# FNet mixing beside a ReLU MLP on one Trainium2 core: two neighbouring quarters of the second transform's operands made in one step each, and the order of block 8 to the end written anew

## The chip, the cores and the metric

The kernel runs on one core of a Trainium2 chip. Its five engines each take their instructions in the order in which they were issued, and wait for one another through semaphores: TensorE (PE; its weight loads are shown as PEld), VectorE (DVE), ScalarE (ACT), GpSimd (POOL) and SyncE (SP). In this kernel SP and POOL only issue DMAs, except for some reductions on POOL. The metric is the device time of one execution in microseconds; three runs of the kernel before took 1236.45, 1238.53 and 1238.07 us, with a median of 1238.07 us.

## The reference

The input x has 2048 rows of 576 numbers. It is normalised along its rows (xn), and the output is the sum of x, of the real part of a two-dimensional Fourier transform of xn, and of a two-layer perceptron with 4608 hidden units:

```python
a = einsum("bsd,ed->bse", xn, dft_hid_re)            # hidden transform
b = einsum("bsd,ed->bse", xn, dft_hid_im)
y = einsum("ts,bse->bte", dft_seq_re, a) - einsum("ts,bse->bte", dft_seq_im, b)
h = maximum(einsum("bsd,df->bsf", xn, w1), 0)
out = x + y + einsum("bsf,fd->bsd", h, w2)
```

The transforms are given as dense matrices, and the kernel works them out as matrix products.

## The kernel before

Every matrix product of two float32 operands is made of three float16 passes. An operand v is split into a high part, which ACT makes by a rounding copy, and a low part, which DVE makes as v minus the high part; the passes are high by high, high by low and low by high. Nearly all products also go through a 2 by 2 block scheme with seven products in place of eight (Strassen's, in Winograd's form): besides the four blocks of an operand it needs sums of blocks, which DVE makes, and its results are added up as they leave PSUM.

The work comes in nine blocks of the perceptron (0 to 8), in which the weights, the hidden layer and the second product of one ninth of the hidden units are worked through. In the last of them the operands of the transforms are prepared too. Behind it comes the hidden transform, whose results stay in the chip as sixteen 128-row tiles (they are taken in two turns of eight), and then the sequence transform in sixteen units of seven products each, eight units after either turn.

The order from block 8 to the end isn't left to a scheduler. It stands in two strings of words, `BLOCK8` and `TURN`; each word names a step and its arguments, the program runs through them one after the other, and so the order of the words is the order of the instructions on each engine. The steps of which the texts speak are these; lines are those of the kernel before.

- `p:g:i:n` seven-product matmuls of the first layer (PE, L710); `f` brings a product out of its bank, `h` and `l` make the high (ACT, L719) and low part (DVE, L723) of the hidden layer, `r` applies the ReLU to a sum block (L739), `x` and `y` make sums of blocks (DVE, L743 to L745 and L748), `H` and `L` the high (ACT, L751) and low part (DVE, L757) of these sums.
- `m:g:n` is product n of the second layer for group g: 12 matmuls of 128x288 (PE, L807). `e:g:n` brings it out: `:A` on ACT (L821), `:V` on DVE (L823), others as an addition on DVE (L825). `a` adds the result to the output in memory by a DMA from POOL (L832).
- `F` loads a block of the sequence matrix (SP, L1229) and `S` takes its column sums of magnitudes (ACT, L1236); `dl` loads the hidden transform's matrix for its maxima (SP, L348), which `dx` takes (DVE, L392). `dh` and `dw` make high (ACT, L1200) and low parts (DVE, L1206) of the hidden transform's operands.
- `q:t:z:n` is product n of the hidden transform for tile t (7 matmuls of 128x288; PE, L1389), and `c:t:z:n` collects it into a buffer of float32 blocks `tb` (DVE, L1402; ACT, L1404).
- A tile in `tb` has four 288-wide blocks b11, b12, b21, b22. `sh:t:s` and `sl:t:s` write the high part (ACT, L1358) and low part (DVE, L1362) of them as operands `R` of the sequence transform: s is 11, 21 or 22 for one block of 288, and 0 for the four sums together (1152). `rs:t` makes these four sums in place (DVE, L1368 to L1371), in which the blocks are overwritten; so `sh` and `sl` of 11, 21 and 22 come before it, those of 0 after it.
- `cl:n:q` loads a block of the sequence matrix for unit n, `os` makes sums of these blocks (DVE, L1444), `oh:m` and `ol:m` make the high (ACT, L1013) and low part (DVE, L1017) of left operand number m. `u:n:i:h` is half h of product i of unit n: 12 matmuls of 128x288 (PE, L1475), over four tiles; half 0 takes the tiles 0, 2, 1, 3 and half 1 the tiles 4, 6, 5, 7. Unit 0's product i uses operand number i. `ue` brings a product out (L1487 to L1491), `ua` writes it out by a DMA.

For each tile half of a product the three matmuls are, in this order, high by high, high (left) by low (R), and low (left) by high (R):

```python
for k in range(HK)[ks]:
    r = right_of(kh * HK + RANK[k])
    for j, (a, c) in enumerate(((0, 0), (0, 1), (1, 0))):
        nc.tensor.matmul(ps, w[:, a, RANK[k]], r[:, c, RIGHT[rq]], ...)
```

Of the kernel before, what the change touches and what calls it, by code (L numbers as in the profile page):

```python
# [9 lines left out]
F16 = mybir.dt.float16  # L10
# [4 lines left out]
ALU = mybir.AluOpType  # L15
# [3 lines left out]
P = 128  # L19
S = 2048  # L20
# [21 lines left out]
SB = 2 * EH  # L42
# [98 lines left out]
p:31:1:4 l:31:1:11 h:31:1:22 a:30:1 dl:0 e:30:3:V F:32:0 p:32:0:1 f:31:1:3 h:31:1:12 l:31:1:12  # L141
r:31:1 m:30:4 f:32:0:1:V f:32:0:2 L:31:0 p:32:0:6 e:30:4 p:32:0:5 f:32:0:6:A l:31:1:22 a:30:4
m:30:5 x:31:1 y:31:1 f:32:0:5:A m:30:6 H:31:1 e:30:5 a:30:5 L:31:1 p:32:0:3 h:32:0:11 dl:1
p:32:1:1 l:32:0:11 dx:0:0 p:32:1:2 e:30:6:V S:32:0 m:31:0 dx:0:1 a:30:6 F:32:1 f:32:0:3 p:32:0:7
f:32:1:1:V r:32:0 f:32:1:2 p:32:1:6 h:32:1:11 f:32:0:7 l:32:1:11 h:32:0:22 p:32:1:5 x:32:0
f:32:1:6:A p:32:1:7 l:32:0:22 e:31:0:A m:31:1 f:32:1:5:V f:32:1:7 h:32:1:22 l:32:1:22 p:32:1:4
e:31:1 p:32:1:3 h:32:1:12 a:31:1 dl:2 l:32:1:12 m:31:3 f:32:1:3 dx:1:1 r:32:1 x:32:1 p:32:0:4
dx:1:0 p:33:0:5 h:32:0:12 m:31:2 l:32:0:12 f:33:0:5:A y:32:0 y:32:1 H:32:0 p:33:0:1 e:31:2:V
S:32:1 p:33:1:1 f:33:0:1:V L:32:0 e:31:3:A m:31:4 F:33:0 H:32:1 f:33:1:1:V m:31:5 e:31:4 L:32:1
a:31:4 dl:3 m:31:6 e:31:5 dx:2:1 a:31:5 m:32:0 e:31:6:V S:33:0 dx:2:0 a:31:6 p:33:1:6 F:33:1  # L150
m:32:1 f:33:1:6:V p:33:0:3 p:33:0:2 p:33:0:6 f:33:0:2 e:32:0:A p:33:1:2 f:33:0:6:V dL:0:0
h:33:0:11 f:33:0:3 m:32:2 f:33:1:2 r:33:0 e:32:1 h:33:1:11 l:33:1:11 a:32:1 p:33:0:7 l:33:0:11
dx:3:1 p:33:1:7 f:33:0:7 m:32:3 x:33:0 h:33:0:22 e:32:2:A l:33:0:22 dx:3:0 p:33:0:4 p:33:1:5
y:33:0 h:33:0:12 dR:0 l:33:0:12 H:33:0 m:32:4 f:33:1:5:V dp:0 S:33:1 f:33:1:7 L:33:0 p:34:0:1
e:32:3:A dL:0:1 p:33:1:4 f:34:0:1:A e:32:4 dh:0:0:1 p:33:1:3 h:33:1:12 dw:0:0:1 a:32:4 h:33:1:22
m:32:5 l:33:1:12 dh:0:0:0 f:33:1:3 F:34:0 r:33:1 dw:0:0:0 p:34:0:5 e:32:5 m:32:6 l:33:1:22
a:32:5 ds:0:0 dh:0:1:1 m:33:0 dh:0:1:0 dw:0:1:1 dh:0:0:2 x:33:1 p:34:0:6 e:32:6:A p:34:0:2
dh:0:0:3 f:34:0:5:V a:32:6 dw:0:0:2 m:33:1 dw:0:0:3 S:34:0 f:34:0:2 dL:0:2 p:34:0:3 f:34:0:6:V
# [118 lines left out]
def kernel(  # L277
# [44 lines left out]
    NS = 7  # L322
# [1279 lines left out]
```

## Time and profile before

| | |
|---|---|
| runs | 1236.45, 1238.53, 1238.07 us (median 1238.07) |
| profiled execution | 1237.58 us, of which the span from the first to the last instruction is 1235.8 us |
| mean granted clock of TensorE | 0.999 |
| busy | PE 1211.6 us (98%), DVE 1061.7 us (86%), ACT 722.7 us (58%), POOL 213.6 us (17%) |

The profile comes from one execution of its own. A busy time is the sum over an engine's instructions, as the profiler recorded them; weight loads of PE overlap its matmuls. In a timeline a row gives the start, the duration, the engine, the line, the operation with the tiles that it writes and reads, the shapes, the number of like instructions that the row stands for, and in brackets the time for which the engine stood idle ahead of it with what ended that. Numbers at the end of buffer names are left out there. Times count from the first instruction.

### The profile page before, as it was taken

The numbers are of one execution on the slowest core, as the hardware profiler recorded it, in microseconds if no ns is written. First come the engines' busy times: TensorE is split into PE (matmuls) and PEld (weight loads), VectorE is DVE, ScalarE is ACT, GpSimd is POOL, SyncE is SP. The second block draws the span as 40 slices with busy tenths as digits, with TensorE's granted clock in tenths as the row PEclk, the third lists the DMA queues.
The fourth block names the chain that finished last, engine by engine and source line by source line (L and its number), as shares of the span: only waits on it lengthen the run. The fifth ranks groups of instructions, "written<-read, shape, count | busy, mean of one in ns | idle before, by whom it ended". The sixth has DMA issues, their size and how long they took to land.

```text
span 1235.8 us, 26013 instructions
## 1 busy us (share of the span) xinstructions
PE 1211.6 (98%) x10394; PEld 993.7 (80%) x10394; DVE 1061.7 (86%) x2046; ACT 722.7 (58%) x1256; POOL 213.6 (17%) x279
## 2 busy tenths in 40 slices
PE   6999999999999999999999999999999999999998
PEld 6856878888888888888888888877777777777777
DVE  7967999988898888988988889999977769987885
ACT  6665776765766666667667546666444445534342
POOL 2641112122213122222121111100111110000000
PEclk9999999999999999999999999999999999999999
DMA  7997468778777778676667577630755532255441
GB/s 227 206 183 171 152 136 169 166 138 164 151 164 142 173 140 181 134 145 139 141 129 156 129 182 165 122 96 26 210 121 142 122 91 49 78 168 173 147 131 35
DMA packets 127050, 175.96 MB, mean 142 GB/s; under 512 B 48336, under 2 KB 88784, under 8 KB 126928
## 3 DMA queue, kind: packets, MB, share of 16 engines
q1 hardware_dynamic: 97696, 121.99, 33.5%
q0 software_dynamic: 28672, 51.92, 28.4%
q8 instruction: 81, 1.33, 0.4%
q10 hardware_dynamic: 560, 0.39, 0.1%
q14 instruction: 41, 0.34, 0.1%
HBM read 112.53 MB, written 56.62 MB: 137 GB/s over the span
## 4 chain that ended last, share of the span: by engine, by line
PE 87%; DVE 6%; DMA 2%; issue 2%; ACT 1%; POOL 1%; SPq 1%; POOLq 0%; DVEq 0%; ACTq 0%
PE bank L710 26%; PE p L807 26%; PE p L1475 26%; PE pd L1389 7%; PE p L847 1%; PE p L586 1%; DMA raw_w<-in_w_dram 1%; DVE R L1362 1%; DMA accs<-in_x_dram 1%; DMA x<-in_x_dram 0%; DMA xT<-wbuf 0%; DVE st L471 0%; DVE wbuf L923 0%; ACT dbuf L511 0%; DVE cs L1017 0%
## 5 line engine op out<-in xcount | busy, mean ns | idle before, releaser
L807 PE MATMUL p<-w2s,h 128*128 128x288 f16 x2688 | 357.1, 286 | 0.6 <-ACT dbuf L821 0.6
L1475 PE MATMUL p<-R,cs 128*128 128x288 f16 x2688 | 331.0, 286 | 2.5 <-DVE cs L1017 2.5
L1475 PEld LDWEIGHTS <-cs 128*128 128x128 f16 x2688 | 262.8, 98 | 69.6 <-DVE cs L1017 3.4
L807 PEld LDWEIGHTS <-h 128*128 128x128 f16 x2688 | 263.0, 98 | 62.8 <-issue 0.8
L710 PEld LDWEIGHTS <-dbuf 128*128 128x128 f16 x1568 | 153.2, 98 | 24.8 <-issue 4.7
L710 PEld LDWEIGHTS <-wbuf 128*128 128x128 f16 x1568 | 153.4, 98 | 20.3
L1013 ACT ACTIVATE cs<-tb,sc_c 128x1024 f16<-128x1024 f32 x56 | 64.3, 1148 | 82.4 <-PE p L1475 58.0
L710 PE MATMUL bank<-xT,dbuf 128*128 128x256 f16 x896 | 109.9, 273 | 1.2 <-ACT accs L700 1.0
L710 PE MATMUL bank<-xT,wbuf 128*128 128x256 f16 x896 | 110.3, 273 | 0.0
L1017 DVE SCALAR_TENSOR_TENSOR cs<-tb,sc_c,cs 128x1024 f16<-128x1024 f32 x56 | 71.7, 1283 | 22.2 <-ACT cs L1013 21.4
L832 POOL DMA_DIRECT2D spill<-dbuf x70 | 61.1, 913 | 166.9 <-DVE dbuf L825 124.0
L710 PE MATMUL bank<-accs,dbuf 128*128 128x256 f16 x672 | 85.9, 273 | 2.4 <-DVE accs L734 1.7
L710 PE MATMUL bank<-accs,wbuf 128*128 128x256 f16 x672 | 85.9, 273 | 0.0
L1013 ACT ACTIVATE cs<-accs,sc_c 128x1024 f16<-128x1024 f32 x40 | 45.9, 1147 | 58.5 <-PE p L1475 45.7
L757 DVE TENSOR_TENSOR h<-s,h 128x1024 f16<-128x1024 f32 x64 | 77.4, 1217 | 2.1 <-ACT h L751 2.1
L751 ACT ACTIVATE h<-s 128x1024 f16<-128x1024 f32 x64 | 66.6, 1049 | 9.8 <-DVE s L748 9.8
L719 ACT ACTIVATE h<-accs 128x256 f16<-128x256 f32 x128 | 51.2, 411 | 34.0 <-DVE accs L734 27.4
L1236 ACT ACTIVATE f<-f 128x1024 f32<-128x1024 f32 x64 | 67.2, 1050 | 3.7 <-DMA f<-in_cim_dram 3.4
L832 POOL DMA_DIRECT2D spill<-wbuf x42 | 39.8, 947 | 156.6 <-DVE wbuf L825 126.5
L700 ACT ACTIVATE accs<-bank 128x256 f32<-128x256 f32 x99 | 37.6, 380 | 44.7 <-PE bank L710 18.2
L1017 DVE SCALAR_TENSOR_TENSOR cs<-accs,sc_c,cs 128x1024 f16<-128x1024 f32 x40 | 51.2, 1281 | 13.7 <-ACT cs L1013 13.3
L821 ACT ACTIVATE dbuf<-p,c_ub 128x576 f32<-128x576 f32 x61 | 45.0, 737 | 27.1 <-PE p L807 27.1
(225 smaller groups left out, 1888.8 us busy)
## 6 DMA issues: line engine op xcount, KB each, us to landing
spill<-dbuf POOLq DMA_DIRECT2D x80, 288.0 KB, 4.5
f<-in_cre_dram SPq DMA_DIRECT2D x32, 512.0 KB, 4.4
f<-in_cim_dram SPq DMA_DIRECT2D x32, 512.0 KB, 5.0
spill<-wbuf POOLq DMA_DIRECT2D x48, 288.0 KB, 5.4
raw_w<-in_w_dram SPq DMA_DIRECT2D x18, 576.0 KB, 4.4
raw_w<-in_w_dram SPq DMA_DIRECT2D x17, 512.0 KB, 4.6
accs<-in_cim_dram SPq DMA_DIRECT2D x16, 512.0 KB, 4.3
tb<-in_cre_dram SPq DMA_DIRECT2D x16, 512.0 KB, 4.3
```

Source lines behind the costliest of these rows:

```text
L710: nc.tensor.matmul(ps, l, r, start=first and m == 0, stop=m == len(todo) - 1, skip_group_check=not first,)
L719: nc.scalar.activation(next(high_low(q)), SOURCE[q], AF.Relu)
L751: order["s"] = nc.scalar.activation(next(high_low(SUMS)), stage_of(slice(1, 5)), AF.Copy).ins
L757: order["lo"] = nc.vector.tensor_tensor(lo, stage_of(slice(1, 5)), hi, ALU.subtract).ins
L807: nc.tensor.matmul(ps[:, c], h[:, x, qa, c * P : (c + 1) * P], w[:, y, qb], start=first and i == 0 and j == 0, stop=i == NQ - 1 and j == 2 ...
L821: freed(nc.scalar.activation(o, ps, AF.Copy, scale=us[b]))
L832: nc.gpsimd.dma_start(spill[g, row, col], sums[g, row, col], accum_op=ALU.add)
L1013: nc.scalar.activation(hi, src, AF.Copy, scale=s)
L1017: nc.vector.scalar_tensor_tensor(lo, src, s, hi, ALU.mult, ALU.subtract)
L1236: nc.scalar.activation(f, f, AF.Abs, scale=2.0**-10, accum_out=sums_c[:, n, q : q + 1])
L1389: nc.tensor.matmul(ps, x[:, k, c * P : (c + 1) * P], dsp[z][:, a, y], start=first and m == 0, stop=m == len(PASSES) - 1, skip_group_check= ...
L1475: nc.tensor.matmul(ps, w[:, a, RANK[k]], r[:, c, RIGHT[rq]], start=first and k == 0 and j == 0, stop=k == HK - 1 and j == 2, skip_group_ch ...
```

## The change

The two blocks b21 and b22 lie side by side in `tb` and in `R`. The step `21` now covers both: one copy of 576 on ACT in place of two of 288, and one subtraction of 576 on DVE in place of two of 288; the words `sh:t:22` and `sl:t:22` are gone. In `part_sums` the first two subtractions (b12 - b11 and b22 - b12) become one of 576, and the last two stay. Over the sixteen tiles that takes away 16 instructions of ACT and 32 of DVE. The strings `BLOCK8` and `TURN` are written anew; some evictions and collections change between ACT and DVE in that. The matmuls are the same ones. At the kernel's start the operand of some idle matmuls lies in another buffer, and they write another bank. Behind `BLOCK8` the changed kernel's line numbers are two lower, and from `part_sums` on three.

```diff
-p:31:1:4 l:31:1:11 h:31:1:22 a:30:1 dl:0 e:30:3:V F:32:0 p:32:0:1 f:31:1:3 h:31:1:12 l:31:1:12
+dl:0 f:31:1:3 m:30:4 e:30:3:A l:31:1:11 m:30:5 e:30:4 dx:0:0 e:30:5 h:31:1:22 L:31:0 p:32:0:5
...
-    idle = stages[:, NS - 1].rearrange("p r k c -> p (r k c)")[:, :P]
+    idle = dbuf[:, 2 * W1B + 2 * SB :].bitcast(F16)[:, :P]
...
-            nc.tensor.matmul(Q[3][:, :P], idle, idle, start=True, stop=True)
+            nc.tensor.matmul(XY[1][:, 1, :P], idle, idle, start=True, stop=True)
...
-    PART = {RB11: (RB11, 0), RB21: (RB21, 2), RB22: (RB22, 3), RT1: (slice(RT1, RT2 + 1), slice(0, 4))}
+    PART = {RB11: (RB11, 0), RB21: (slice(RB21, RB22 + 1), slice(2, 4)), RT1: (slice(RT1, RT2 + 1), slice(0, 4))}
...
-        b11, b12, b21, b22 = (v[:, j] for j in range(4))
-        tt(b11, b12, b11, ALU.subtract)
-        tt(b12, b22, b12, ALU.subtract)
+        b11, b21, b22 = (v[:, j] for j in (0, 2, 3))
+        tt(v[:, :2], v[:, 1::2], v[:, :2], ALU.subtract)
         tt(b22, b22, b11, ALU.subtract)
         tt(b21, b21, b22, ALU.subtract)
...
-    S_ = {"11": RB11, "21": RB21, "22": RB22, "0": RT1}
+    S_ = {"11": RB11, "21": RB21, "0": RT1}
```

Three places of the new order are shown. The first is DVE in the last group of the perceptron, group 35. `h8_3_1` is the second half of its hidden layer, and `s8_3_1` holds that half's sums of blocks. Before, from the eviction `e:34:4` on; the L723 row is the word `l:35:1:11`:

```order
L825 SCALAR_TENSOR_TENSOR sums_9806<-p2_8_2_0_10328,c_ub_8989,sums_9806 128x576
L723 SCALAR_TENSOR_TENSOR h8_3_1_10463<-accs_98,h8_3_1_10463 128x256
L736 TENSOR_TENSOR s8_3_1_10482<-bank3_1753,s8_3_1_10482 128x256
L734 TENSOR_TENSOR accs_98<-bank1_1751,accs_98 128x256
L743 SCALAR_TENSOR_TENSOR s8_3_1_10482<-accs_98,s8_3_1_10482 128x256
L744 SCALAR_TENSOR_TENSOR s8_3_1_10482<-accs_98,s8_3_1_10482 128x256
L745 SCALAR_TENSOR_TENSOR s8_3_1_10482<-accs_98,s8_3_1_10482 128x256
L825 SCALAR_TENSOR_TENSOR sums_9806<-p2_8_2_3_10428,c_ub_8989,sums_9806 128x576
```

And in the changed kernel, from the same eviction `e:34:4` on; the L721 rows are `l:35:1:11` and `l:35:1:12`:

```order
L823 SCALAR_TENSOR_TENSOR sums_9823<-p2_8_2_0_10293,c_ub_8989,sums_9823 128x576
L741 SCALAR_TENSOR_TENSOR s8_3_1_10410<-accs_98,s8_3_1_10410 128x256
L742 SCALAR_TENSOR_TENSOR s8_3_1_10410<-accs_98,s8_3_1_10410 128x256
L743 SCALAR_TENSOR_TENSOR s8_3_1_10410<-accs_98,s8_3_1_10410 128x256
L746 SCALAR_TENSOR_TENSOR s8_3_0_10322<-bank0_1750,s8_3_0_10322 128x256
L823 SCALAR_TENSOR_TENSOR sums_9823<-p2_8_2_3_10447,c_ub_8989,sums_9823 128x576
L746 SCALAR_TENSOR_TENSOR s8_3_1_10410<-bank1_1751,s8_3_1_10410 128x256
L1204 SCALAR_TENSOR_TENSOR wbuf_97<-dbuf_96,c_sdm_9921,wbuf_97 32x2x288
L1204 SCALAR_TENSOR_TENSOR wbuf_97<-accs_98,c_sdm_9921,wbuf_97 32x288
L1204 SCALAR_TENSOR_TENSOR wbuf_97<-raw_dk1_0_10403,c_sdm_9921,wbuf_97 128x288
L721 SCALAR_TENSOR_TENSOR h8_3_1_10479<-accs_98,h8_3_1_10479 128x256
L721 SCALAR_TENSOR_TENSOR h8_3_1_10479<-bank1_1751,h8_3_1_10479 128x256
```

The word `l:35:1:11`, which stood right behind `e:34:4`, now stands behind `e:34:5` (the second L823 row, which reads the product `m:34:5`) and three words `dw`. On PE the product `m:35:0` (tile `p2_8_3_0`) is the first to use it. Its first weight loads of `h8_3_1` in the changed kernel:

```order
L805 LDWEIGHTS h8_3_1_10479
L805 MATMUL p2_8_3_0_10543<-w2s8_1_8909,h8_3_1_10479 128x288
L805 LDWEIGHTS h8_3_1_10479
L805 MATMUL p2_8_3_0_10543<-w2s8_1_8909,h8_3_1_10479 128x288
L805 LDWEIGHTS h8_3_1_10479 [waits DVE_49]
L805 MATMUL p2_8_3_0_10543<-w2s8_1_8909,h8_3_1_10479 128x288
```

The sixth weight load of the product is the first to read a low part of `h8_3_1`, and it now has a wait for DVE of its own, which the row before did not have.

The second place is ACT in the same stretch. Before, from the first `dh` there to the evictions `e:35:0` and `e:35:2`, which stand as one row:

```order
L1200 ACTIVATE wbuf_97<-raw_dk1_1_10423,c_sdm_9920 128x288
L1200 ACTIVATE wbuf_97<-raw_dk1_0_10357,c_sdm_9920 128x288
L1200 ACTIVATE wbuf_97<-raw_dk1_1_10423,c_sdm_9920 128x2x288
L1200 ACTIVATE wbuf_97<-raw_dk1_0_10357,c_sdm_9920 128x2x288
L1200 ACTIVATE wbuf_97<-accs_98,c_sdm_9920 128x288
L751 ACTIVATE h8_3_1_10463<-s8_3_1_10482 128x1024
L821 ACTIVATE sums_9806<-p2_8_3_0_10538,c_ub_8989 128x576 x2
```

In the changed kernel, from `H:35:0` to the same two evictions:

```order
L749 ACTIVATE h8_3_0_10350<-s8_3_0_10322 128x1024
L819 ACTIVATE sums_9823<-p2_8_2_0_10293,c_ub_8989 128x576
L749 ACTIVATE h8_3_1_10479<-s8_3_1_10410 128x1024
L1234 ACTIVATE f15_3_10328,sums_c_1749<-f15_3_10328 128x1024
L1198 ACTIVATE wbuf_97<-raw_dk1_0_10403,c_sdm_9921 128x2x288
L1198 ACTIVATE wbuf_97<-raw_dk1_1_10528,c_sdm_9921 128x288
L1198 ACTIVATE wbuf_97<-raw_dk1_1_10528,c_sdm_9921 128x2x288
L819 ACTIVATE sums_9823<-p2_8_3_0_10543,c_ub_8989 128x576 x2
```

The sums of magnitudes (`S:35:1`, L1234) and three `dh` now stand between `H:35:1` and the evictions; before, they all came ahead of `H:35:1`.

The third place is DVE at the handover from the hidden to the sequence transform, in the first turn. `R4` to `R7` are the operands of tiles 4 to 7, and `cs2`, `cs3`, `cs0` the left operands that `ol:2`, `ol:3` and `ol:4` finish. Before:

```order
L1362 TENSOR_TENSOR R4_11061<-tb_10713,R4_11061 128x1152
L1362 TENSOR_TENSOR R6_11101<-tb_10713,R6_11101 128x1152
L1402 SCALAR_TENSOR_TENSOR tb_10713<-pd5_0_0_11071,tb_10713 128x288
L1402 SCALAR_TENSOR_TENSOR tb_10713<-pd5_0_2_11073,tb_10713 128x288
L1362 TENSOR_TENSOR R5_11173<-tb_10713,R5_11173 128x288
L1362 TENSOR_TENSOR R7_11228<-tb_10713,R7_11228 128x288 x3
L1368 TENSOR_TENSOR tb_10713<-tb_10713 128x288
```

Behind these rows stood the other seven subtractions of `rs:5` and `rs:7`, `ol:2`, `sl:5:0`, `sl:7:0` and `ol:3`. In the changed kernel:

```order
L1360 TENSOR_TENSOR R5_11237<-tb_10735,R5_11237 128x576
L1360 TENSOR_TENSOR R6_11129<-tb_10735,R6_11129 128x1152
L1366 TENSOR_TENSOR tb_10735<-tb_10735 128x576
L1367 TENSOR_TENSOR tb_10735<-tb_10735 128x288
L1368 TENSOR_TENSOR tb_10735<-tb_10735 128x288
L1366 TENSOR_TENSOR tb_10735<-tb_10735 128x576
L1367 TENSOR_TENSOR tb_10735<-tb_10735 128x288
L1368 TENSOR_TENSOR tb_10735<-tb_10735 128x288
L1015 SCALAR_TENSOR_TENSOR cs2_11252<-c0_10740,sc_c_9398,cs2_11252 128x1024
L1360 TENSOR_TENSOR R5_11237<-tb_10735,R5_11237 128x1152
L1360 TENSOR_TENSOR R4_11082<-tb_10735,R4_11082 128x1152
L1360 TENSOR_TENSOR R7_11235<-tb_10735,R7_11235 128x1152
```

The 1152-wide low parts of tiles 6 and 4 stood ahead of the last collections; the one of tile 6 now comes behind all 21-steps, and the one of tile 4 behind `ol:2`.

More of the change, by code (lines that the diff above doesn't have):

```diff
@@ L147 @@
[L147 to L158, printed above, removed]
@@ new lines @@
+u:2:5:1 u:2:6:0 u:2:6:1 u:3:0:0 u:3:0:1 u:3:1:0 ua:1:1 ua:1:6 ua:1:4 os:3:1 ua:2:1 oh:24
+ue:2:6:V oh:23 ol:23 ol:24 cl:4:2 os:3:3 os:3:2 u:3:1:1 ue:3:0:A oh:25 oh:26 cl:4:1 ue:2:5
+cl:5:0 cl:4:3 ol:25 u:3:2:0 ol:26 u:3:2:1 oh:27 ue:3:2:V u:3:3:0 u:3:3:1 u:3:4:0 u:3:4:1
+ue:3:3:V ol:27 ue:3:1 oh:28 oh:29 ue:3:4 os:4:0 ol:28 u:3:5:0 os:4:1 ol:29 u:3:5:1 u:3:6:0
+u:3:6:1 cl:5:2 oh:30 oh:31 ue:3:5 ol:30 u:4:0:0 ua:2:4 ua:2:6 os:4:2 ol:31 os:4:3 u:4:0:1
+u:4:1:0 cl:5:1 ua:3:4 u:4:1:1 ue:4:0:A ue:3:6:A ua:3:1 ua:2:5 ua:3:5 u:4:2:0 u:4:2:1 u:4:3:0
@@ L273 @@
+oh:107 ue:14:5 ol:107 ua:14:5 u:14:6:1 u:15:0:0 ue:14:6 oh:108 ua:14:6 ol:108 u:15:0:1 os:15:3
+u:15:1:0 ue:15:0 oh:109 u:15:1:1 ol:109 u:15:2:0 oh:110 ue:15:1 ol:110 u:15:2:1 u:15:3:0 ue:15:2
+oh:111 ua:15:2 ol:111 u:15:3:1 u:15:4:0 ue:15:3 u:15:4:1 u:15:5:0 ue:15:4 ua:15:4 u:15:5:1
+u:15:6:0 ue:15:5 ua:15:5 u:15:6:1 ue:15:6 ua:15:6
 """
```

230 lines of the change are left out of this document (115 added, 115 removed).

## The prediction

> **What bounds the kernel now.** I read the page first, for the shares of the engines, then stretches of the span, since a share says nothing of a stage. Columns of the second fence: the stretch, its length, then the busy time and instructions of PE, PEld, DVE, ACT and POOL, the granted clock, the DMA share, GB/s.
>
> ```profile
> span 1235.8 us, 26013 instructions
> ...
> PE 1211.6 (98%) x10394; PEld 993.7 (80%) x10394; DVE 1061.7 (86%) x2046; ACT 722.7 (58%) x1256; POOL 213.6 (17%) x279
> ```
>
> ```profile
> 690.00:840.00 150.00, 150.00 (x1269) 123.80 (x1268) 136.40 (x277) 87.84 (x167) 22.39 (x27) 1.00 0.64 139
> 840.00:860.00 20.00, 18.07 (x144) 13.80 (x143) 19.54 (x40) 13.64 (x25) 0.00 (x0) 1.00 0.00 1
> 860.00:880.00 20.00, 18.55 (x150) 14.31 (x148) 19.79 (x21) 9.16 (x10) 3.44 (x4) 1.00 0.71 206
> 880.00:1220.00 340.00, 340.00 (x2778) 271.58 (x2776) 276.36 (x332) 150.50 (x176) 23.92 (x28) 1.00 0.45 122
> ```
>
> PE bounds nearly everything: from 690 us, where block 8's order begins, to the end it never stands still, but for 840 to 880 us. There DVE is busy for 39.3 of 40 us, and PE loses 1.93 + 1.45 = 3.4 us. So the change can win at most about these 3.4 us (and 1 us more that the matmuls' modelled ends cover, below), and can lose whatever its order makes PE wait elsewhere. A DVE instruction saved where DVE has time to spare is worth nothing. The waits of PE over 690 to 1236 us (total, times, longest) are all at that handover:
>
> ```profile
> PE p L1475 <- DVE cs L1017: 2.5, 3, 1.1
> PE pd L1389 <- DVE tb L1402: 0.8, 1, 0.8
> ```
>
> The timeline of the handover, PE alone:
>
> ```profile
> 849.64 1.02 PE L1389 MATMUL pd<-wbuf,accs 128*128 128x288 f16 x7
> 850.73 1.02 PE L1389 MATMUL pd<-dbuf,xT 128*128 128x288 f16 x7
> 852.54 1.02 PE L1389 MATMUL pd<-dbuf,accs 128*128 128x288 f16 x7 [0.79 <-DVE tb L1402]
> 853.40 4.82 PE L1475 MATMUL p<-R,cs 128*128 128x288 f16 x38
> 859.27 3.18 PE L1475 MATMUL p<-R,cs 128*128 128x288 f16 x24 [1.05 <-DVE cs L1017]
> 863.00 3.11 PE L1475 MATMUL p<-R,cs 128*128 128x288 f16 x24 [0.55 <-DVE cs L1017]
> 867.01 8.26 PE L1475 MATMUL p<-R,cs 128*128 128x288 f16 x66 [0.90 <-DVE cs L1017]
> ```
>
> The first three rows are the products `q:5:1:4`, `q:5:0:3` and `q:5:0:4`, the last of the first turn. The stops of the last three rows end with `ol:2`, `ol:3` and `ol:4`, the low parts without which a product of unit 0 can't go on. Matmuls of 288 start 0.1225 us apart (66 of them in 8.26 us, less the tail of the last), so 7 take 0.86 and 12 take 1.47 us. From 849.64 us, without a wait, three q products (2.6) and nine halves of unit 0's products 0 to 4 (13.2) would end at 865.4; with 22 matmuls of the last row still theirs they end at 867.01 + 2.7 = 869.7. So the handover costs 4.3 us now, and 4.4 with the short wait ahead of the first row: 1.2 in the q products, the rest ahead of `ol:2` to `ol:4`.
>
> **The change, part by part.** *The merged steps.* Their prices:
>
> ```profile
> L1362 DVE TENSOR_TENSOR R<-tb,R 128x1152 f16<-128x1152 f32 x8 | 10.6, 1350 | 0.0
> ...
> L1362 DVE TENSOR_TENSOR R<-tb,R 128x288 f16<-128x288 f32 x24 | 10.1, 450 | 0.4 <-ACT R L1358 0.2
> ```
>
> ```profile
> 852.77 1.55 DVE L1362 TENSOR_TENSOR R<-tb,R 128x288 f16<-128x288 f32 x4
> 854.25 0.45 DVE L1368 TENSOR_TENSOR tb<-tb 128x288 f32<-128x288 f32 x1
> 854.73 0.46 DVE L1369 TENSOR_TENSOR tb<-tb 128x288 f32<-128x288 f32 x1
> ```
>
> A width of 576 isn't in these groups; the line through 288 (450) and 1152 (1350) gives 1.04 ns an element, so 0.75 us. Back to back the next instruction starts earlier than the end: four of L1362 in 1.55 us, so 0.37 us apart, and on the same line 0.67 us for 576: a merged low part saves 2 x 0.37 - 0.67 = 0.07 us of DVE. The sums wait for each other's result, 0.48 us apart; two become one of 0.75 + 0.04, which saves 0.96 - 0.79 = 0.17. Together 0.24 us a tile, some 2 us a turn of eight tiles; at the least 0 (if the strided operand of the merged subtraction costs what the second instruction did), at the most 0.3 (two durations of 450 for one of 750, twice). On ACT it saves about 0.1 us a tile beside other work. In the second turn, behind 880 us, PE has no wait, so nothing is won there. In the first, DVE is the late one, and the 2 us would count if the order left the chain as it was.
>
> [...]
>
> *The last perceptron group, order of DVE.* PE's matmuls are the same ones, and I expect the waits of the new order up to here to be covered. Rows of PE and of DVE:
>
> ```profile
> 790.09 4.57 PE L807 MATMUL p<-w2s,h 128*128 128x288 f16 x36
> ```
>
> ```profile
> 786.74 0.41 DVE L723 SCALAR_TENSOR_TENSOR h<-accs,h 128x256 f16<-128x256 f32 x1
> ...
> 789.52 0.82 DVE L825 SCALAR_TENSOR_TENSOR sums<-p,c_ub,sums 128x576 f32<-128x576 f32 x1
> 790.26 0.42 DVE L723 SCALAR_TENSOR_TENSOR h<-accs,h 128x256 f16<-128x256 f32 x1
> 790.59 0.42 DVE L748 SCALAR_TENSOR_TENSOR s<-bank,s 128x256 f32<-128x256 f32 x1
> 790.93 0.80 DVE L1206 SCALAR_TENSOR_TENSOR wbuf<-dbuf,c_sdm,wbuf 32x576 f16<-32x576 f32 x1
> ...
> 794.06 0.51 DVE L1206 SCALAR_TENSOR_TENSOR wbuf<-accs,c_sdm,wbuf 32x288 f16<-32x288 f32 x1
> 794.50 0.50 DVE L1206 SCALAR_TENSOR_TENSOR wbuf<-raw_dk,c_sdm,wbuf 128x288 f16<-128x288 f32 x1
> ```
>
> The PE row is `m:34:6`, `m:35:0` and `m:35:1`, so `m:35:0` starts at 790.09 + 1.47 = 791.56 us, then and now. The first DVE row is `l:35:1:11`, done at 787.15, 4.4 us ahead of `m:35:0`. Now it stands behind `e:34:5`, `y:35:1` and three `dw`. `e:34:5` waits for `m:34:5`, which now stands directly ahead of `m:34:6` and so ends at 790.25 us (the start of that, and the tail of a matmul). From there, by distances between starts: eviction 0.74, `y` 0.34, `dw` of 576 0.73, two `dw` of 288 at 0.44 each, and the low part itself 0.41: 790.25 + 3.1 = 793.35 us. PE wants it for the sixth weight load, 791.56 + 5 x 0.1225 = 792.17 us. A wait of about 1.2 us (take 1.25 with the semaphore). Bounds: 0, if the wait for `e:34:5` is shorter than I read it; 1.7, if each step costs its duration (0.82 + 0.42 + 0.80 + 0.51 + 0.50 + 0.41 = 3.46) and the next product's low part is late as well.
>
> *The same group, order of ACT.* `m:35:2` is to write over the sum that `e:35:0` brings out. Before, that eviction came right behind `H:35:1`; now `S:35:1` and three `dh` stand between.
>
> ```profile
> L1404 ACT ACTIVATE tb<-pd 128x288 f32<-128x288 f32 x30 | 11.7, 405 | 7.2 <-PE pd L1389 6.3 <-DVE wbuf L1206 0.5 <-DVE R L1362 0.3
> L751 ACT ACTIVATE h<-s 128x1024 f16<-128x1024 f32 x11 | 11.6, 1052 | 2.4 <-DVE s L748 2.4
> L821 ACT ACTIVATE sums<-p,c_ub 128x576 f32<-128x576 f32 x14 | 10.3, 734 | 7.1 <-PE p L807 7.1
> L1358 ACT ACTIVATE R<-tb 128x288 f16<-128x288 f32 x24 | 10.0, 437 | 7.5 <-DVE tb L1402 7.4
> L1236 ACT ACTIVATE f<-f 128x1024 f32<-128x1024 f32 x9 | 9.4, 1047 | 2.8 <-DMA f<-in_cim_dram 2.8
> L1358 ACT ACTIVATE R<-tb 128x1152 f16<-128x1152 f32 x8 | 9.3, 1159 | 3.1 <-DVE tb L1371 3.1
> ...
> L1200 ACT ACTIVATE wbuf<-raw_dk,c_sdm 128x576 f16<-128x576 f32 x6 | 4.3, 765 | 0.5 <-DVE raw_dk L943 0.5
> ```
>
> `e:34:6` (now on ACT) waits for `m:34:6` and can't start before 791.7; 0.73, then 1.05, 1.2 (1.05 and the read of its accumulator), three `dh` of 0.77, some 0.5 and 0.77, and 0.73 end at 797.5 us, and at 797.0 if each starts some 0.07 ahead of the end before it, as in the rows of DVE above. PE, 1.25 late, and with `m:35:0`, `m:35:1` and one q product (1.47 + 1.47 + 0.86) comes at 796.6. So 0.4 us more; from 0 to 0.8.
>
> *The handover.* Let R be the end of `q:5:1:4`, which is some 850 us in either order. Before, the 1152-wide low parts of tiles 4 and 6 stood ahead of the last collections. Now ACT makes `sh:5:21` as its last copy of a block, ending at R + 2.94: a collection of 0.41, copies of 0.44, 0.44 and 0.68 (576, between 437 and 1159), a collection and a copy of 0.68 more, less 0.1 of overlap. DVE then takes, in order, `sl:5:21` (to R + 3.65), `sl:6:0` (1.25), `rs:5` and `rs:7` (1.65 each: 0.79 + 0.49 + 0.37), so that `ol:2` runs from R + 8.2 to R + 9.5; then `sl:5:0`, `sl:4:0`, `sl:7:0`, `ol:3`, both sums `os`, and `ol:4` to R + 18.25. PE does the last q product and four halves, is at the third matmul of `u:0:2:0` by R + 6.8 (0.86 + 4 x 1.47 + 0.1), and waits there 2.7 us (`ol:2` ends at R + 9.5); then for `sl:4:0` 1.35, for `ol:3` 0.7, for `ol:4` 0.85: 5.6 us in all, against 4.4 now, so +1.2. Without `sl:6:0` and `sl:4:0` in that place `ol:2` to `ol:4` would each come 1.25 to 2.5 us sooner, and 1.6 us of waits would be left, so the end of this term that favours the change is -2.8; the other is +2.
>
> *The rest.* The units behind 880 us and the second turn have slack of 0.05 to 0.2 us in the new order at some places; up to +0.2 together, taken as nothing, covered by the half product of 1.47 in front of each. Where that cover is gone, a unit waits for one low part more, 1.3 us. The idle matmuls' other bank: nothing, since PE waits there for x in either case; otherwise the 0.1 us of a matmul.
>
> *The sum.* 1.25 + 0.4 + 1.2 = +2.85 us on the profiled 1237.58, so 1240.4. The median of the runs is 0.5 above the profiled execution: 1240.9.
>
> **The rivals.** *The merges shorten the chain that PE waits for (faster).* If DVE runs ahead of the place that I give it, because the 2 us saved by the merges have already moved its whole queue, `sl:6:0` and `sl:4:0` fall into gaps, the handover costs 1.6 in place of 4.4, and the waits of group 35 are small too: 1238.07 - 2.8 = 1235.3, up to 0.3 more with these. For it: DVE is busy for 39.3 of 40 us there, so time saved shows at once. Against it: the chain begins with an ACT copy that waits for a PE product, and no saving ahead of that moves it. It decides if `ol:2` ends by R + 7.
>
> *Some of the waits are covered.* One of the two kinds is real (group 35 or the handover), the other comes out at nothing: 1238.07 + 0.8 to 1.7, about 1239.2. For it: each is a small difference of two sums of many rows.
>
> *A late load in block 8.* The changed order has SP issue `dl:2` ahead of `F:32:1`; before it was the other way round.
>
> ```profile
> 711.58 0.34 SPq L1229 DMA_DIRECT2D f<-in_cim_dram  x1
> 714.13 0.55 SPq L348 DMA_DIRECT2D raw_d<-in_dft_dram  x1
> ```
>
> ```profile
> DMA to landing us min/median/max: 3.6/4.6/8.6
> ```
>
> The last row is of L348's loads. `dl:2` waits for `dx:0:1`; behind it the load of `F:32:1` starts about 714.7 and, sharing the queues, lands between 718.5 and 723.3. `S:32:1`, `H:32:0`, four small steps and the eviction `e:31:2` follow on ACT, 4.1 us, and PE needs that at 726.0, so the limit is 721.9. At worst 1.4 us more, with the other terms 1242.3 to 1243.
>
> **How the numbers follow.** The three runs differ by up to 0.17%, so 0.2%, 2.5 us (1235.6 to 1240.5), is about what can be told from no change. My own case 0.48 (its range 1239.6 to 1242.3, a third of it below 1240.5); some waits covered 0.22; late load 0.10; shorter chain 0.20. Slower: 0.32 of my case, the 0.10, and 0.05 of the covered case where one wait is larger than I read it, 0.47. The same: 0.16, 0.17 and the 0.03 of the shorter chain that lies above the bound, 0.36. Faster: 0.17. The range reaches to 1234.8, where both group 35 is covered and the chain is shortest, which leaves out 0.1, and to 1243.4 on the other side, the late load with the other terms at their size, which leaves out as much.
>
> **What would show it.** Right: PE waits on L805 for DVE (about 1.2 us) at 792 and for ACT (0.4) near 796; at the handover one wait of 2.7 us for L1015, and rows 576 wide with 0.75 us on L1360 and L1366. Wrong: no PE wait near 792; waits of the unit's matmuls (L1472) of under 3 us in sum; a wait of L805 for ACT at 726 behind L1234 with its DMA (the late load); or waits beyond 880 us, where I found none.

## The result, and the profile after

The changed kernel takes 1240.55 us (median of 16 runs, 1239.02 to 1243.12), the kernel before 1238.19 us beside it (16 runs, 1236.45 to 1240.87). The ratio is 1.0020, with a 95% interval of 1.0013 to 1.0028: slower by 2.4 us, 1.6 to 3.5. The profiled execution took 1241.81 us, 1.3 above the median of its runs.

The page, the stretches that answer to those of before, and the waits of PE from 690 us on (total, times, longest) in the changed kernel:

```profile
span 1240.0 us, 25956 instructions
...
PE 1210.6 (98%) x10394; PEld 992.9 (80%) x10394; DVE 1049.5 (85%) x2001; ACT 722.8 (58%) x1253; POOL 215.5 (17%) x279
```

```profile
690.00:840.00 150.00, 148.78 (x1263) 123.00 (x1261) 127.24 (x258) 90.71 (x173) 23.53 (x27) 1.00 0.65 139
840.00:860.00 20.00, 18.02 (x148) 14.26 (x146) 18.75 (x32) 12.64 (x23) 0.00 (x0) 1.00 0.01 1
860.00:880.00 20.00, 18.91 (x138) 14.10 (x138) 17.57 (x17) 9.42 (x11) 0.85 (x1) 0.91 0.71 217
880.00:1220.00 340.00, 338.29 (x2761) 269.95 (x2759) 273.31 (x318) 146.38 (x169) 26.87 (x31) 1.00 0.46 121
```

```profile
PE p L1472 <- ACT accs L1486: 2.5, 2, 2.3
PE pd L1386 <- DVE tb L1403: 1.5, 1, 1.5
PE p L805 <- DVE h L721: 1.1, 1, 1.1
PE p L1472 <- DVE cs L1015: 0.8, 2, 0.6
PE p L805 <- ACT sums L819: 0.2, 1, 0.2
```

DVE is busy for 12 us less, 2.4 to 3.6 us of it for the merge (1061.7 to 1059.3 us in `before_merged` below, 1053.1 to 1049.5 from `after_unmerged` to the changed kernel) and the rest for the other changes of the order, and in the 40 us of the handover for 36.3 us where it was 39.3. PE gains nothing from it: it now stands still in 690 to 840 us (1.2 us) and behind 880 us (1.7 us), where it did not before. A granted clock below 1.00, 0.91 in 860 to 880 us, is new too.

The part of the kernel ahead of this order differs from execution to execution: in the fourteen traces of this document, the 4000th matmul starts between 461.8 and 467.2 us. Behind it, two executions of one order agree to 0.01 us in the two pairs that can be compared (the kernel before and `before_fill`, `best` and `best_old_idle`). So beside the runs I use the *path*: the time from that matmul's start to the last one's, and in it the waits, as the time between two neighbouring starts less the usual 0.1225 us (0.109 for 256 wide). A profile's wait is up to 0.17 us shorter, since its matmuls' ends are modelled. Worked out from the matmul records, without waits the path is 763.0 us in both kernels:

```
                         before   changed
path                     768.2    772.0
all waits on it            5.2      9.0
  group 35                 0        1.5   (1.23 at 793.5 us, 0.31 at 797.0)
  handover                 4.4      5.2   (changed: waits 2.43, 0.32, 0.81 and 1.7 of slow clock)
  second turn              0        2.0   (0.40 at 1007.6, 1.64 at 1016.8)
  smaller ones             0.8      0.2
```

The rows behind the first two lines of waits, PE at the last group and at the handover:

```profile
788.69 3.72 PE L805 MATMUL p<-w2s,h 128*128 128x288 f16 x29
793.48 2.50 PE L805 MATMUL p<-w2s,h 128*128 128x288 f16 x19 [1.07 <-DVE h L721]
...
796.99 4.57 PE L805 MATMUL p<-w2s,h 128*128 128x288 f16 x36 [0.15 <-ACT sums L819]
```

```profile
851.98 6.04 PE L1472 MATMUL p<-R,cs 128*128 128x288 f16 x48
860.29 5.02 PE L1472 MATMUL p<-R,cs 128*128 128x288 f16 x26 [2.27 <-ACT accs L1486]
865.46 3.12 PE L1472 MATMUL p<-R,cs 128*128 128x288 f16 x24 [0.16 <-DVE cs L1015]
869.23 15.98 PE L1472 MATMUL p<-R,cs 128*128 128x288 f16 x129 [0.65 <-DVE cs L1015]
```

Twenty-six matmuls in 5.02 us in the second of these rows, where 24 take 3.12 in the next, show that PE's granted clock was at half for a time (0.50 in 861 to 863 us; the last section has its windows); the text calls this the slow clock. And the merged steps on DVE, 805 to 876 us:

```profile
L1366 DVE TENSOR_TENSOR tb<-tb 128x576 f32<-128x576 f32 x8 | 6.0, 752 | 0.4 <-ACT tb L1401 0.4
L1360 DVE TENSOR_TENSOR R<-tb,R 128x576 f16<-128x576 f32 x8 | 5.9, 754 | 0.1
```

### The profile page after: what moved, and what is told of

It is laid out like the page before. It is cut to its first block, busy times and chain, and to the rows that moved or that the text cites. A ratio compares the mean times of both kernels' runs of the same rounds, so it can differ in the third digit from the quotient of the medians.

```text
span 1240.0 us, 25956 instructions
## 1 busy us (share of the span) xinstructions
PE 1210.6 (98%) x10394; PEld 992.9 (80%) x10394; DVE 1049.5 (85%) x2001; ACT 722.8 (58%) x1253; POOL 215.5 (17%) x279
## 4 chain that ended last, share of the span: by engine, by line
PE 84%; DVE 6%; DMA 3%; ACT 2%; issue 2%; POOL 1%; SPq 1%; ACTq 0%; POOLq 0%; DVEq 0%
PE bank L708 26%; PE p L805 26%; PE p L1472 25%; PE pd L1386 7%; DMA raw_w<-in_w_dram 1%; DVE cs L1015 1%; DVE R L1360 1%; DMA xT<-wbuf 1%; DMA accs<-in_x_dram 1%; DVE st L469 0%; SPq L662 0%; DMA x<-in_x_dram 0%; DVE tb L1441 0%; DVE wbuf L921 0%; ACT dbuf L509 0%
## 5 line engine op out<-in xcount | busy, mean ns | idle before, releaser
L1234 ACT ACTIVATE f<-f 128x1024 f32<-128x1024 f32 x64 | 67.2, 1050 | 2.4 <-DMA f<-in_cim_dram 2.4
```

The source lines that it names most:

```text
L1234: nc.scalar.activation(f, f, AF.Abs, scale=2.0**-10, accum_out=sums_c[:, n, q : q + 1])
```

## The experiments

Time and ratio are those of the runs (the ratio to the kernel before on the same chip, with its 95% interval), the path is from the one profiled execution of each kernel.

```
                  median us  before   ratio (95%)              path
changed             1240.55  1238.19  1.0020 (1.0013, 1.0028)  772.00
l_early             1240.91  1237.56  1.0026 (1.0017, 1.0036)  772.00
l_e_early           1243.97  1237.56  1.0047 (1.0032, 1.0061)  776.93
os_early            1239.25  1237.56  1.0014 (1.0004, 1.0024)  770.14
before_merged       1237.68  1237.56  0.9997 (0.9988, 1.0006)  767.86
after_unmerged      1240.73  1237.24  1.0034 (1.0021, 1.0046)  772.48
order_mended        1238.09  1237.24  1.0003 (0.9995, 1.0012)  769.19
merged_ue           1236.63  1237.24  0.9999 (0.9990, 1.0007)  767.43
before_fill         1236.97  1237.24  0.9996 (0.9987, 1.0006)  768.23
mended_low_early    1236.19  1237.67  0.9986 (0.9977, 0.9995)  768.03
merged_ue_pool      1239.45  1237.67  1.0012 (1.0001, 1.0022)  772.31
best                1236.34  1237.76  0.9992 (0.9984, 1.0001)  768.01
best_old_idle       1237.16  1237.76  0.9996 (0.9987, 1.0005)  768.01
before                                                         768.23
```

### What the merge is worth by itself

`before_merged` has the kernel before's order, with one word for the two, which stands where the later of the two stood:

```diff
-    PART = {..., RB21: (RB21, 2), RB22: (RB22, 3), ...}
+    PART = {..., RB21: (slice(RB21, RB22 + 1), slice(2, 4)), ...}
-        tt(b11, b12, b11, ALU.subtract)
-        tt(b12, b22, b12, ALU.subtract)
+        tt(v[:, :2], v[:, 1::2], v[:, :2], ALU.subtract)
```

> The kernel before with the merged steps alone: of each pair of words for 21 and 22 the later one makes both, and the rest of the order is as before. Theory A (DVE is busy without a gap from 838 us to the end of the handover, so that what the merges save ahead of it shows at its end): ol:4 comes 1.5 to 2 us sooner after the last q product's nominal time, the handover costs some 2.5 us in place of 4.4, time 1.5 to 2 us below the kernel before. Theory B (the chain begins with the last copies behind q:5:1:4, so only the two last tiles' merges count): 0.5 us faster. Theory C (the merged step stands at the place of the later word and moves work toward the handover): no gain, up to 0.5 us slower.

The path is 0.4 us shorter, by the runs no difference. Waits in `before_merged`:

```profile
PE p L1474 <- DVE cs L1017: 2.4, 3, 0.9
PE pd L1388 <- ACT tb L1403: 0.5, 1, 0.5
PE pd L1388 <- DVE tb L1401: 0.2, 1, 0.2
```

The three waits for `ol:2` to `ol:4` (2.5 us before) are still there; the last q products wait less, and the wait for `ol:2` is 0.14 us shorter. What DVE is spared ahead of the handover shows in `merged_ue` (below): its order is the same up to there, and its execution stands within 0.2 us of the one before, so that the window holds the same work (that of `before_merged` runs 3 us late).

```profile
690.00:840.00 150.00, 150.00 (x1270) 123.80 (x1268) 135.27 (x268) 86.78 (x162) 22.48 (x27) 1.00 0.65 139
```

DVE is busy for 135.27 us where it was 136.40. These 1.1 us become idle time of DVE, since PE stands still there in neither kernel. Over the whole turn, from the matmul at 690 us to the one that waits for `ol:4`, DVE's busy time falls by 1.6 us (163.4 to 161.7 in `before_merged`), and the path by 0.4. Theory B held on the path, with 0.4 us for its 0.5, and A fell; that the chain starts anew with the last collections is B's reading of it, which no run tests by itself.

`after_unmerged` takes the merge out of the changed kernel's order:

```diff
-... sl:4:21 ...            (and each other sh and sl of 21)
+... sl:4:21 sl:4:22 ...
```

> The changed kernel's order with the merge undone: each sh and sl of 21 is followed at once by one of 22, and rs has four subtractions again. Theory B (the chain of the handover is anchored behind the last q products, and DVE has idle time ahead of that, so only the last two tiles' merges count): the last low part of unit 0's wait comes about 0.5 to 0.6 us later (0.07 x 2 for the low parts and 0.17 x 2 for the sums, and some on ACT's copies), the rest of the order has the same waits; 0.5 to 1 us slower than the changed kernel. Theory A (every saved piece of DVE time counts): 2 us slower at the handover and up to 2 us more in the second turn.

The path is 0.5 us longer, with the same waits at the same places, and 2.66 us for the first of the handover in place of 2.43. Both kernels agree: the merge is worth some 0.4 to 0.5 us of path in either order, not 2, and it does not cause the loss. The runs can't tell the merged and the unmerged kernel apart in either order.

### The last perceptron group

`l_early`:

```diff
-... e:34:3:A e:34:4 r:35:1 ... dw:1:0:1 l:35:1:11 l:35:1:12 S:35:1 ...
+... e:34:3:A l:35:1:11 e:34:4 r:35:1 ... dw:1:0:1 l:35:1:12 S:35:1 ...
```

> The changed kernel with one word moved: l:35:1:11 again ahead of e:34:4, where DVE stood idle for 0.66 us. Theory A (the two waits of group 35 are one after the other, behind one chain on ACT): the wait of m:35:0 for DVE (1.07 us) goes, but the eviction e:35:0 still ends at about 796.9 us, behind S:35:1 and three dh, so m:35:2 waits for it 1.2 to 1.4 us in place of 0.15; time as the changed kernel, within 0.3 us. Theory B (the waits add up, as the prediction summed them): 1.1 us faster than the changed kernel.

The wait of `m:35:0` is gone, the path is the same to 0.01 us, and `m:35:2` waits in its place (1.56 us between starts). In `l_early`:

```profile
PE p L805 <- ACT sums L819: 1.4, 1, 1.4
```

So it is one chain, that of ACT, which costs 1.5 us; the wait for DVE only came first and covered most of it. Taking one of them away is worth nothing.

`l_e_early` moves the eviction too, in a place that brings a new wait:

```diff
-... S:35:1 dh:1:0:0 dh:1:1:1 a:34:4 a:34:5 m:35:0 m:35:1 dh:1:1:0 e:35:0:A ...
+... m:35:0 e:35:0:A S:35:1 dh:1:0:0 dh:1:1:1 a:34:4 a:34:5 m:35:1 dh:1:1:0 ...
```

> The same word moved, and m:35:0 with e:35:0 ahead of S:35:1 and the dh in the table, so that the eviction comes right behind H:35:1 on ACT. Both theories: neither wait in group 35 is left (below 0.2 us in sum), unless the dh that now come 0.7 us later make the hidden transform's first products wait; 1.0 to 1.2 us faster than the changed kernel, so about 1239.4 where that has 1240.55.

The expectation failed: the path is 4.9 us longer. `e:35:0` now stands ahead of `a:34:4`, whose block lies in the same buffer, and overwrites it, so this kernel leaves one block of group 34's results out. The additions wait behind it, and the next evictions for them. In `l_e_early`:

```profile
792.88 2.61 POOL L829 DMA_DIRECT2D spill<-sums  x3 [11.75 <-ACT sums L818]
...
797.06 0.82 DVE L822 SCALAR_TENSOR_TENSOR sums<-p,c_ub,sums 128x576 f32<-128x576 f32 x1 [1.92 <-DMA spill<-sums]
...
797.93 2.14 PE L804 MATMUL p<-w2s,h 128*128 128x288 f16 x12 [2.43 <-DVE sums L822]
```

Between starts, the two pauses are 2.60 and 1.26 us, 2.3 us more than the two of the changed kernel. The other 2.7 us are a slow clock behind the first of them, in the window from 801 to 806 us:

```profile
801.00:806.00 5.00, 5.00 (x23) 3.17 (x23) 3.17 (x6) 3.40 (x5) 0.00 (x0) 0.53 0.18 34
```

The run says nothing on the two theories. `order_mended`, below, makes the same room in another way: it takes `S:35:1` from in front of the eviction.

### The second turn

`os_early`:

```diff
-... u:6:6:1 ue:6:6:V ue:6:5 os:7:0 os:7:1 ...
+... u:6:6:1 os:7:0 os:7:1 ue:6:6:V ue:6:5 ...
```

> The changed kernel with os:7:0 and os:7:1 ahead of ue:6:6 and ue:6:5 on DVE. Theory A (one cause: the sums of unit 7 stand behind two evictions that wait for the end of u:6:6, and everything on ACT and DVE behind them is late): both waits go, 0.23 us at 1007.6 and 1.47 us for c:8:0:1 at 1016.8; 1.6 to 2.0 us faster than the changed kernel. Theory B (the collection c:8:0:1 is late for its own place behind ol:54 and ol:55): only the first wait goes and the second stays above 1 us; 0.3 to 0.5 us faster.

Both waits are gone but for 0.18 us, and the path is 1.9 us shorter: one cause, theory A. In the changed kernel the sums of unit 7 stood behind two evictions that wait for the end of `u:6:6`; ACT waited for the sums, the evictions and high parts of unit 7 came late on ACT, the low parts `ol:54` and `ol:55` late on DVE, and behind these the collection `c:8:0:1`, without which the second turn's `q:8:0:6` had no bank. The changed kernel, DVE and then PE:

```profile
1013.90 2.47 DVE L1015 SCALAR_TENSOR_TENSOR cs<-tb,sc_c,cs 128x1024 f16<-128x1024 f32 x2
1016.29 0.45 DVE L1403 TENSOR_SCALAR tb<-pd 128x288 f32<-128x288 f32 x1
```

```profile
1016.80 1.02 PE L1386 MATMUL pd<-dbuf,accs 128*128 128x288 f16 x7 [1.47 <-DVE tb L1403]
```

### The three places together, and the handover

`order_mended` has the edits of `l_early` and `os_early`, and `S:35:1` in a gap of ACT:

```diff
-... f:35:1:3 e:34:3:A ... l:35:1:12 S:35:1 dh:1:0:0 ...
+... f:35:1:3 S:35:1 e:34:3:A ... l:35:1:12 dh:1:0:0 ...
```

> The changed kernel with three places of the order mended: l:35:1:11 ahead of e:34:4, S:35:1 ahead of e:34:3 (into 1.29 us in which ACT stands idle there), os:7:0 and os:7:1 ahead of ue:6:6 and ue:6:5. The three waits that were named (group 35's two, which exclude each other, and the second turn's) go: from the sum of the matmul starts, 1.5 + 2.0 us off the changed kernel's path, so equal to the kernel before within 0.5 us, with the handover's 0.9 us the only thing left. If the rival holds that something outside these places costs time, it stays 1 us or more above the kernel before.

The path is 2.8 us shorter than the changed kernel's and 1.0 longer than that of the kernel before; by the runs the two are equal (1.0003). What is left is 0.5 us at `m:35:2` and the handover: waits of 5.24 us there against 4.36. `mended_low_early` then does what the prediction named as the handover's cause the other way round:

```diff
-... sl:4:21 c:5:0:7 ... sh:6:0 os:0:1 ... c:5:1:3 rs:4 c:5:1:2 sl:5:11 ... sh:5:21 sh:4:0 sl:7:21 sl:5:21 sl:6:0 u:0:0:0 ... sl:5:0 sl:4:0 u:0:0:1
+... sl:4:21 rs:4 c:5:0:7 ... sh:6:0 sh:4:0 os:0:1 ... c:5:1:3 sl:6:0 c:5:1:2 sl:4:0 sl:5:11 ... sh:5:21 sl:7:21 sl:5:21 u:0:0:0 ... sl:5:0 u:0:0:1
```

> The mended order with the 1152-wide low parts of tiles 4 and 6 (sl:4:0, sl:6:0, with rs:4 and sh:4:0) moved ahead of the steps of the last collections, as the kernel before has them. The prediction's step (their place behind the last collections is what the handover's extra wait comes from): the wait for a low part of R (0.95 us) goes and that for ol:2 falls by up to 1.25 us, 0.9 us or more off the mended order, so at or below the kernel before. The rival (DVE is the engine that is short here, whatever the order: its work between the last products and ol:4 is the same, and only its idle time ahead of that is lost): the last q products wait for collections in its place, and ol:4 comes no more than 0.3 us sooner; time as the mended order within 0.3 us.

The prediction's step held in part: the wait for a low part of R is gone, the handover's waits fall from 5.24 to 3.97 us, the path by 1.2 us, and the last q products wait for 0.1 us at most. The first of the three waits did not shrink, though (2.45 us): `ol:2`, and the eviction `ue:0:0` that PE waits for by the profile, come at the same time behind `q:5:1:4` as in `order_mended`, although `sl:4:0` now stands ahead of `ol:2` too; DVE's 0.8 us of idle time there took most of that up. So what was won lies behind it, and the 1.6 us of waits that the prediction had left without the two low parts in that place did not come. In `mended_low_early`:

```profile
PE p L1471 <- ACT accs L1485: 2.3, 1, 2.3
PE p L1471 <- DVE cs L1014: 1.2, 2, 0.6
PE p L804 <- ACT sums L818: 0.4, 1, 0.4
```

The kernel is faster than the one before by the runs (0.9986, 0.9977 to 0.9995), and so than the changed one; on the path behind the start it is ahead by only 0.2 us, so that most of the 1.5 us in the runs is not explained by the order. `best` swaps one more pair, `dh:1:1:0 e:35:0:A` to `e:35:0:A dh:1:1:0`:

> The mended order with the low parts of tiles 4 and 6 early, and e:35:0 one dh (0.7 us) sooner on ACT. The wait of m:35:2 for that eviction (0.5 us) goes; the handover is left as it was (2.45, 0.7 and 0.8 us). From the sum of the matmul starts 0.5 us off the path of the kernel with the low parts early, so 0.6 to 0.7 us below the kernel before behind the start; by the runs 1 to 2 us below it.

The expectation of 0.5 us failed. Its path is the same to 0.02 us: the 0.5 us at `m:35:2` became 0.3 there and 0.3 three products later. So `mended_low_early` and `best` stand for the same kernel, at 1.4 to 1.5 us below the one before in the runs; the interval of the second reaches 1.0001.

### The kernel before, with ACT and POOL taking work from DVE

`merged_ue` is `before_merged` with `ue:0:2:V` made `ue:0:2:A`.

> The kernel before with the merged steps and one eviction more on ACT (ue:0:2, 0.43 us of DVE between ol:3 and ol:4). The wait for ol:4 falls by 0.4 us, the rest is as with the merged steps alone: 0.4 us below that, so 0.5 to 0.9 us below the kernel before. If ACT's queue is what sets ol:4 (the eviction stands ahead of oh:4 there), no gain.

The path falls by 0.4 us as expected, to 767.43 us, the shortest of all; the runs can't tell it from the kernel before (0.9990 to 1.0007). `merged_ue_pool` gives two sums to POOL besides:

```diff
-        tt(o, a, b, op)
+        (nc.gpsimd.tensor_tensor if n == 0 and k < 2 else tt)(o, a, b, op)
```

> The kernel before with the merged steps, ue:0:2 on ACT, and the first two sums of unit 0 (os:0:0 and os:0:1, 1.22 us each on DVE at 838 to 843 us) on POOL, which stands idle there; by POOL's subtraction of 512 float32 (1.27 us) some 2.5 us each, needed only at oh:2, ten microseconds later. If DVE's backlog there reaches the handover: the waits of the last q products (0.6 and 0.35 us) go, and ol:2 to ol:4 come sooner; 1 us below the kernel with ue:0:2 alone, and about 1.8 us below the kernel before on the path behind its start. If the chain is anchored behind the last q products: those two waits go at most, 0.3 to 0.6 us. If POOL's sums hold up DVE, no gain.

It is slower: by 4.9 us than `merged_ue` on the path of the profiled execution, which was the slowest of its twelve (1244.48 us), and by 1.5 us than the kernel before in the runs (1.0001 to 1.0022). While POOL makes the sums, two operations of DVE with both operands outside PE's banks take 2.7 and 2.3 times as long as alone. POOL and DVE in `merged_ue_pool`:

```profile
837.37 2.36 POOL L1443 TENSOR_TENSOR accs<-accs 128x1024 f32<-128x1024 f32 x1 [28.00 <-PE pd L1388]
839.80 3.21 POOL L1443 TENSOR_TENSOR c<-accs,c 128x1024 f32<-128x1024 f32 x1
```

```profile
837.35 3.46 DVE L1017 SCALAR_TENSOR_TENSOR cs<-accs,sc_c,cs 128x1024 f16<-128x1024 f32 x1
840.73 0.45 DVE L1401 SCALAR_TENSOR_TENSOR tb<-pd,tb 128x288 f32<-128x288 f32 x1
841.10 3.12 DVE L1362 TENSOR_TENSOR R<-tb,R 128x1152 f16<-128x1152 f32 x1
```

Alone the first and the third of these take 1.28 and 1.35 us. The collection between them, which reads a bank of PE's results, took its usual 0.45 us. ACT's next collection waits for the second low part, and PE for that collection, 3.35 us between starts; the clock is slow behind this pause, which costs 1.7 us more:

```profile
844.77 1.25 PE L1388 MATMUL pd<-dbuf,accs 128*128 128x288 f16 x7 [3.19 <-ACT tb L1403]
```

```profile
845.00:849.00 4.00, 4.00 (x21) 2.61 (x19) 1.05 (x3) 1.81 (x4) 0.00 (x0) 0.57 0.00 0
```

That the other executions lose less would fit a slow clock that comes in some of them only; no run shows it.

### The idle matmuls of the start

`before_fill` is the kernel before with the two lines on the idle matmuls, `best_old_idle` is `best` without them.

> The kernel before with the idle matmuls' new operand and bank alone. The prediction's view: no difference (within 0.3 us). The rival: the start of the kernel changes, since the idle matmuls no longer share a bank or buffer with what follows; 0.5 to 1 us either way.

> The same kernel with the idle matmuls at its start as the kernel before has them (operand and bank). If they make no difference, as the prediction has it: equal to it within 0.3 us, in runs and on the path behind the start. If the changed kernels' start is quicker for them: 0.5 to 1 us slower, with the difference ahead of the 4000th matmul.

On the path there is no difference in either pair (768.23 and 768.23, 768.01 and 768.01). In the runs the changed start is ahead by 0.3 us in the first pair and 0.8 in the second, neither clear of the noise (the interval of the first takes in 1, those of the second pair overlap). The other kernels point the same way. In the eight with the changed start, `l_e_early` aside, the runs' ratio gives 0 to 1.5 us less over the kernel before than the path does; in the three with the old start, `merged_ue_pool` aside, from 0.3 less to 0.7 more. Whether the new operand and bank make the start some tenths quicker stays open even so; it would explain why the changed kernel loses 3.8 us on the path and 2.4 (1.6 to 3.5) in the runs.

## Why the prediction was right, and where not

- **Time and sign.** Forecast 1240.9 us and slower, measured 1240.55. The sum came out, but not all of its terms: 1.25 + 0.4 + 1.2 were forecast on the path, 1.5 + 0.9 + 2.0 were found, less 0.6 of smaller waits that went. That the total is so close is partly luck: a term of 2.0 us was missed, and the runs show 2.4 us where the path shows 3.8.
- **What bounds.** Right: PE from end to end, with the handover as its only loss before.
- **The merged steps.** Sizes right: 0.75 us forecast for 576 wide, 0.752 and 0.754 measured; `rs` 1.65 us. The prediction's 2 us a turn came out as 1.6 us of DVE's busy time. What they are worth was hedged rightly (nothing in the second turn), but "the 2 us would count if the order left the chain as it was" was wrong: with the order left, 0.4 us. Of the 1.6 us, 1.1 are spared ahead of 840 us and turn into idle time of DVE.
- **DVE in group 35.** Right in place, engine and size: low part due at 793.35 us, done at 793.43, and PE goes on at 793.48; wait of 1.25 forecast, 1.07 in the profile, 1.23 between starts.
- **ACT in group 35.** Right cause, 0.4 forecast, 0.15 to 0.31 measured. What the sum got wrong is that the two are not two costs: `l_early` takes the first away and the second grows to 1.56.
- **The handover.** Size about right, cause right in part: +1.2 forecast, +0.9 measured, and `mended_low_early` shows that the place of the low parts of tiles 4 and 6 costs 1.2 us of path. `ol:2` was forecast for 9.5 us and `ol:4` for 18.25 behind R, the end of `q:5:1:4`; they came 9.1 and 17.9 behind it. But the first wait, 2.7 forecast and 2.43 measured, is not the one for `ol:2` that the prediction had at the third matmul of `u:0:2:0`. PE stands at the first one, behind 48 matmuls (four halves), and waits for the eviction `ue:0:0`, which stands on ACT behind `sh:5:0`, which waits for `rs:5`, and behind `oh:3`. The changed kernel, ACT and then DVE (`ol:2`):

```profile
857.65 1.16 ACT L1356 ACTIVATE R<-tb 128x1152 f16<-128x1152 f32 x1 [1.72 <-DVE tb L1368]
858.72 1.13 ACT L1011 ACTIVATE cs<-accs,sc_c 128x1024 f16<-128x1024 f32 x1
859.76 0.48 ACT L1486 ACTIVATE accs<-p,us_c 128x288 f32<-128x288 f32 x1
```

```profile
859.12 1.28 DVE L1015 SCALAR_TENSOR_TENSOR cs<-c,sc_c,cs 128x1024 f16<-128x1024 f32 x1
```

  The eviction ends at 860.24 us and PE goes on at 860.29; `ol:2` ends at 860.40, ahead of the third matmul at 860.59. Two chains behind the sums `rs:5` and `rs:7` end 0.16 us apart, and the prediction followed one of them. The three waits forecast behind it (1.35, 0.7, 0.85) show in `os_early` as 1.3, 0.7 and 0.8; in the changed kernel's trace the slow clock fills most of the first two.
- **The rest: wrong.** "The units behind 880 us and the second turn have slack of 0.05 to 0.2 us in the new order at some places; up to +0.2 together, taken as nothing" is the step that failed: 2.0 us were lost there, and waits beyond 880 us were one of the prediction's own signs of being wrong. It took the half product in front of each place as cover, and did not follow what comes late behind `ue:6:6`: the sums of unit 7 on DVE, then the high parts on ACT, the low parts `ol:54` and `ol:55`, and the collection queued behind them.
- **Rivals.** No late load: PE runs on over 726 us without a wait, as the row below has it. The shorter chain fell with `before_merged`, and with the changed kernel, whose merge is worth 0.5 us and whose `ol:2` ended 9.1 us behind R, not by 7. That some of the waits are covered fell too: group 35 cost 1.5 us and the handover 0.9.

```profile
723.55 4.57 PE L805 MATMUL p<-w2s,h 128*128 128x288 f16 x36
```

## What to carry to other kernels

Saved time on an engine that is late only at one place counts there alone from the point where its work is handed to it; ahead of that it becomes idle time, so ask where the chain starts anew before summing savings. When two waits follow one another at one place, take the later of the two chains, not their sum, and take both away or none. After finding an instruction with little slack, follow everything queued behind it on its engine to the next engine that reads it: here a wait of 0.4 us was followed 9 us later by one of 1.6 us with the same cause.

## What the runs showed of the hardware that was not expected

**Behind a pause of 2.4 to 2.7 us PE's clock was halved in four traces of nine.** Nine traces here have the handover's pause of 2.42 to 2.66 us between two matmuls. In four of them (the changed kernel, `l_early`, `l_e_early` and `after_unmerged`) the granted clock fell to about 0.5 for 3 to 4 us behind it; in the other five it stayed at 1.00. The changed kernel and `os_early`, the same pause and order, in the four microseconds behind it:

```profile
860.00:864.00 4.00, 3.71 (x17) 2.41 (x17) 4.00 (x4) 1.29 (x2) 0.00 (x0) 0.57 0.02 4
```

```profile
862.00:866.00 4.00, 2.84 (x22) 2.12 (x22) 4.00 (x4) 1.21 (x2) 0.00 (x0) 1.00 0.01 4
```

It cost nothing in this place: from the end of the pause to the matmul that waits for `ol:4` there are 8.94 us in the one and 8.93 in the other (869.23 - 860.29 and 871.14 - 862.21), because DVE sets that end. Where PE's own products came next, it cost 1.7 us (`merged_ue_pool`, behind 3.35 us) and 2.7 us (`l_e_early`, behind 2.60 us at 798 us). Why the clock fell behind the pause in some traces and not in others is not shown.

**Beside POOL's subtractions two operations of DVE took 2.7 and 2.3 times as long.** A POOL operation on 1024 float32 beside DVE's took the latter from 1.28 to 3.46 and from 1.35 to 3.12 us, while a collection that takes one operand from PE's banks kept its 0.45 us. PE lost 3.35 us in one piece, since the next collection came late on ACT. The spare engine was no spare one. The low part of 837.35 us ends 1.1 us behind POOL's first sum and that of 841.10 us 1.2 us behind its second, each about as long behind as it takes alone (1.28 and 1.35 us). By the records the first low part starts 0.02 us ahead of the first sum, so which of the two came first is not shown, nor what held DVE up.
